# Two attention-and-MLP layers on one core: opening loads reordered, q/k drains shared between two engines, and rules in the instruction scheduler meant to keep ScalarE fed

## The chip, the cores and the metric

The kernel runs on one core of a Trainium2 chip. The metric is the device time of one execution in microseconds (us). A median is taken over the executions of one kernel; "span" is the length of the one execution that was profiled, some 2 us shorter than its time. Engine names: PE is TensorE (matmuls), ACT is ScalarE, DVE is VectorE, POOL is GpSimd, SP is the engine that issues most DMA transfers.

## The reference, cut to what matters

A sequence of 2048 tokens of width 576 passes two layers. Each is sliding-window attention (32 heads of 18, window 256), then an MLP of 4608 hidden units with tanh-gelu, both behind a layer norm and with a residual.

```python
def _A_ref(x, wqkv, wo):                        # attention
    H = 32; Dh = D // H; W = 256
    q, k, v = ...                               # x @ wqkv, split into heads
    scores = jnp.einsum("bhqd,bhkd->bhqk", q, k) * (Dh ** -0.5)
    scores = jnp.where(mask, scores, -1e9)      # causal, at most 256 back
    o = jnp.einsum("bhqk,bhkd->bhqd", _softmax(scores), v)
    return o.reshape(B, S, D) @ wo
def _B_ref(x, w1, b1, w2, b2):                  # MLP
    h = _gelu(x @ w1 + b1)
    return h @ w2 + b2
for _ in range(2):                              # two layers, same weights
    x = x + _A_ref(_layernorm(x), ...)
    x = x + _B_ref(_layernorm(x), ...)
```

## The kernel before

The work is cut into eight chunks of 512 tokens, four per layer. A chunk passes these stages: projections to q, k and v (120 matmuls), eight head groups of scores, exp, mask and weighted sum, the output projection (40 matmuls), a first MLP half and a second MLP half. I call the hidden half of a chunk a gelu block: there are 16 of them, two per chunk, and their order is fixed. Stages of different chunks overlap: while ACT works on one chunk's exps, PE multiplies for another.

The program does not write instructions directly. It adds tasks with an engine, a cost in us, a priority, and what they read and write. A greedy scheduler then places them by a model of time and thereby fixes each engine's instruction order. The kernel hands each engine its instructions in that order, so what waits in a list holds up what stands behind it (the profile after shows DVE standing 3.54 us in this way).

```python
while len(order) < n:                           # Plan.schedule, cut
    best = None
    for e in ENGS:
        for t in released[e]:
            st = max(free[e], t.ready)
            if t.alloc:                         # banks of PSUM it needs
                got, when = place(t)
                ...
                st = max(st, when)
            key = (round(st, 3), t.prio, t.idx) # earliest start first, then priority
            if best is None or key < best[0]:
                best = (key, t, st, got)
    _, t, st, got = best
    if t.eng == "pe" and st < self.warm_until and st - free["pe"] > 0.4:
        self.keep_warm(free["pe"], st, bank_free, extra)   # dummy matmuls into the gap
    ...
```

Scores and exps of one unit (a head group has three units after the first chunk). The scores of four heads fill two pairs of PSUM banks, of which three are open to them; each pair is emptied by one exp on ACT:

```python
add("pe", fn, reads=rd, writes=bs, cost=0.06 + ncol * 0.00053, ..., alloc=bs, fifo="pa", after=[...])
for h2 in range(2):
    add("act", lambda e, h2=h2: e.activation(pT[...], two(bs[h2])[:, :, lo:hi], ACT.Exp, scale=SCALE), ..., fifo="act", prio=prio)
...                                             # masks on POOL, then the weighted sum on PE
```

The opening, for chunk 0. A q or k tile is drained from PSUM in two halves by DVE and then turned by a DMA transpose; the scores wait for those transposes. The value weights, the second chunk's input and the two MLP biases are loaded while this goes on. The 18 KB bias b1 is read element by element into a column layout:

```python
w_load(0); w_load(1)                            # q and k weights; v follows below
for i in range(n0):
    ln_rstd([i], False, -20)
    ln_norm_T(i, i, xnTa, "xa", -6, x_in, [f"xin{i}"], pe=True)
dma("pool", b2bc[:, :], ..., reads=["xa3"], writes=["b2"], ...)
def load_b1(e):
    src = bass.AP(tensor=B_b1.tensor, offset=B_b1.offset, ap=[[1, P], [P, NF], [1, 1]])
    ... e.dma_start(b1col[:, :], src)
add("pool", load_b1, reads=["xa3"], writes=["b1"], dma="b", ...)
w_load(2, ["xa0"])                              # value weights
xin_load(4, 4, ["xa0"], -6)                     # input of the second chunk
for i in range(n0):
    qkv(0, i, -5)
xin_load(8, 4, ["k3"], -4)                      # input of the third chunk

# in qkv: drains of a q or k tile
for o in range(2):
    add("dve", ... e.tensor_copy(qv[:, o * 16:(o + 1) * 16, 0:DH], bank(b)...), reads=[bs[o]], writes=[f"qn{sl}h{o}"], cost=0.42, prio=prio)
add("sp", ... e.dma_start_transpose(dst, qn[:, sl, :]), reads=[f"qn{sl}h0", f"qn{sl}h1"], ...)
```

The softmax here doesn't subtract the row's maximum and nothing guards it: scores larger than these inputs give would overflow.

## Time and profile before

| | before |
|---|---|
| time at the time of the prediction | 958.56 us, median of 3 |
| span of the profiled run | 953.9 us |
| PE busy | 914.3 us |
| ACT busy, 25.8 us (first exp) to 110.3 us (first gelu block) | 58.1 of 84.5 us |
| dummy matmuls | 71 |

First the page's table of busy time (us, share of the span, instructions), its PE part:

```profile
PE 914.3 (96%) x9403; PEld 564.0 (59%) x9403; DVE 313.7 (33%) x804; ACT 590.7 (62%) x709; POOL 369.1 (39%) x507
```

PE is the limit of the kernel as a whole. The Trainium skill, "Trainium Kernel Development and Optimization", section Performance Expectations, calls matmul busy time a bad metric for the distance to the limit, because matmuls are pipelined.

Next the waits of ACT, from the first exp to the first gelu block. The columns are who waited, for whom, us in total, times, and the longest:

```profile
ACT pT L655 <- PE ps L646: 38.6, 27, 12.2
```

12.2 of these 38.6 us lie before the first exp; the other 26.4 are the idle time between exps, always for scores. Then, in the timeline of PE just before the first gelu block (start, us, engine, line, what), the dummies of line 490:

```profile
105.62 1.01 PE L490 MATMUL ps<-warm 128*128 128x256 bf16 x4
...
107.56 1.16 PE L490 MATMUL ps<-warm 128*128 128x256 bf16 x7
108.65 0.40 PE L646 MATMUL ps<-x_res,kT 32*128 32x256 bf16 x8
...
110.27 0.61 PE L771 MATMUL ps<-xnTm,w_sb 64*128 64x512 bf16 x4
```

All projections that could be done were done (400, of which 40 are output projections), so PE waited for exps and ran dummies. They did not hold the full clock: it was 0.69 in 105 to 110 us. The late start of the exps stands in the first exp, in the first score matmul's wait, and in the DMA queues from 8 to 26 us (packets, MB, share of 16 engines; below, issues with KB and median us to landing):

```profile
25.79 1.51 ACT L655 ACTIVATE pT<-ps 128x768 bf16<-128x768 f32 x2 [12.24 <-PE ps L646]
```

```profile
25.40 0.34 PE L646 MATMUL ps<-qT,kT 32*128 32x384 bf16 x4 [2.78 <-DMA qT<-qn]
```

```profile
q0 software_dynamic: 4768, 0.31, 79.8%
...
qT<-qn SPq DMA_TRANSPOSE x4, 5.5
...
b1col<-in_B_b_dram POOLq DMA_DIRECT2D x1, 18.0 KB, 10.3
```

The packets of 0.31 MB of biases, 4768 of them, are under way for 80% of the DMA engines' time in this stretch. Shares of different queues overlap: the hardware queue has 77.1% in the same stretch. Last, the granted PE clock in two stretches of the opening. The columns are stretch, length, then busy us and instructions of PE, PEld, DVE, ACT and POOL, then the clock (0.91 and 0.83), DMA share and GB/s:

```profile
20.00:40.00 20.00, 14.27 (x164) 9.09 (x162) 12.50 (x36) 10.16 (x14) 8.20 (x12) 0.91 1.55 138
40.00:60.00 20.00, 17.77 (x239) 11.17 (x236) 9.63 (x23) 13.74 (x19) 13.69 (x21) 0.83 0.92 191
```

### The profile page before, as it was taken

To read this page: it belongs to the slowest core of one execution; us is meant where nothing else is said; L and a number is where in the kernel's file an instruction comes from. 1 tells how busy PE (TensorE), PEld (TensorE's weight loads), DVE (VectorE), ACT (ScalarE), POOL (GpSimd) and SP (SyncE) were. 2 spreads that over 40 slices of the span, in tenths; PEclk is the share of its full clock that TensorE was granted. 3 is DMA by queue.
4 is the path that set the end of the run, shared out by engine and by line. 5 is a ranking of instruction groups with operands and counts; after the bars stand their busy time and mean duration, and the time that the engine had idled before them with its cause. 6 is when DMAs were issued, how large, how long until landed. Compare 5 with 4: busy or idle time off the path is not lost. (4 is left out here: it accounts for less than half of the span.)

```text
span 953.9 us, 22759 instructions
## 1 busy us (share of the span) xinstructions
PE 914.3 (96%) x9403; PEld 564.0 (59%) x9403; DVE 313.7 (33%) x804; ACT 590.7 (62%) x709; POOL 369.1 (39%) x507
## 2 busy tenths in 40 slices
PE   8799899999999999999999999999999999999998
PEld 6466455564664746655575656747466464656556
DVE  7556301461153412723145221442215220241001
ACT  1676768476836778376744877557784677752541
POOL 4555636164531636225331544315443163620100
PEclk9799999999999999999999999999999999999999
DMA  9898456954098340984259351983519816174540
GB/s 198 145 217 143 96 171 179 200 129 123 27 201 201 93 126 14 219 177 138 75 119 201 90 168 46 176 175 89 182 26 189 193 47 191 36 202 131 161 137 26
DMA packets 240663, 130.10 MB, mean 136 GB/s; under 512 B 158768, under 2 KB 238384, under 8 KB 240560
## 3 DMA queue, kind: packets, MB, share of 16 engines
q1 hardware_dynamic: 231248, 120.96, 54.3%
q0 software_dynamic: 6880, 5.03, 3.5%
q10 hardware_dynamic: 2432, 2.65, 0.9%
q8 instruction: 75, 1.23, 0.5%
q14 instruction: 28, 0.23, 0.1%
HBM read 91.87 MB, written 2.36 MB: 99 GB/s over the span
## 5 line engine op out<-in xcount | busy, mean ns | idle before, releaser
L655 ACT ACTIVATE pT<-ps 128x1024 bf16<-128x1024 f32 (+2 forms) x384 | 347.8, 971 | 118.1 <-PE ps L646 116.9
L676 POOL TENSOR_SCALAR_AFFINE_SELECT pT<-pT 128x512 bf16<-128x512 bf16 (+1 forms) x368 | 278.7, 781 | 278.4 <-ACT pT L655 262.4
L786 ACT ACTIVATE hT<-ps,b1col 128x512 bf16<-128x512 f32 x288 | 197.9, 687 | 215.8 <-PE ps L783 215.1
L811 PE MATMUL ps<-w_sb,hT 128*128 128x288 bf16 x2304 | 314.3, 286 | 4.3 <-DVE x_res L727 2.7
L783 PE MATMUL ps<-xnTm,w_sb 128*128 128x512 bf16 x1152 | 267.3, 381 | 0.0
L811 PEld LDWEIGHTS ps<-w_sb,hT 128*128 128x128 bf16 x2304 | 210.9, 97 | 79.5 <-issue 19.2
L783 PEld LDWEIGHTS ps<-xnTm,w_sb 128*128 128x128 bf16 x1152 | 105.9, 98 | 141.1 <-issue 28.7
L727 DVE TENSOR_TENSOR x_res<-ps,x_res 128x288 f32<-128x288 f32 x160 | 70.6, 449 | 349.3 <-PE ps L811 328.9
L580 PE MATMUL ps<-wqkv,xnTa 128*128 128x288 bf16 x960 | 135.0, 290 | 4.7 <-DVE qn L610 2.0
L580 PEld LDWEIGHTS ps<-wqkv,xnTa 128*128 128x128 bf16 x960 | 88.8, 99 | 37.5 <-DVE qn L610 5.4
L693 PEld LDWEIGHTS ps<-vA,pT 128*128 128x128 bf16 x2880 | 95.0, 96 | 26.2 <-issue 9.4
L693 PE MATMUL ps<-vA,pT 128*128 128x20 bf16 x2880 | 100.0, 172 | 4.3 <-POOL pT L676 2.7
L793 POOL TENSOR_TENSOR x_res<-x_res,b2bc 128x576 f32<-128x576 f32 x32 | 44.9, 1402 | 93.7 <-ACT hT L786 93.7
L646 PE MATMUL ps<-qT,kT 32*128 32x384 bf16 (+2 forms) x1216 | 64.6, 278 | 8.5 <-ACT pT L655 4.8
L610 DVE CAST qn<-ps 128x288 bf16<-128x288 f32 x128 | 58.1, 455 | 39.0 <-PE ps L580 37.9
L512 POOL TENSOR_SCALAR vtmp<-mv_all 128x1 f32<-128x1 f32 (+1 forms) x43 | 8.3, 192 | 142.7 <-DVE mv_all L503 142.2
L580 PE MATMUL ps<-wo_sb,attT 128*128 128x288 bf16 x320 | 42.7, 286 | 7.8 <-DMA attT<-attq 6.5
L501 DVE BATCH_NORM_STATS2 st_all<-x_res 128x6 f32<-128x288 f32 x104 | 44.8, 447 | 13.8 <-DMA x_res<-in_A_x_dram 12.7
L771 PE MATMUL ps<-xnTm,w_sb 64*128 64x512 bf16 x288 | 45.0, 381 | 2.3 <-ACT pT L655 2.2
L730 DVE TENSOR_TENSOR xn<-ps,x_res 128x288 bf16<-128x288 f32 x32 | 14.6, 458 | 97.4 <-PE ps L811 97.4
L646 PEld LDWEIGHTS ps<-qT,kT 32*128 32x128 bf16 x1216 | 19.6, 92 | 39.6 <-issue 23.2
L524 DVE TENSOR_SCALAR xn<-x_res,mv_all,rstd 128x576 bf16<-128x576 f32 x52 | 31.6, 610 | 34.0 <-DMA xnTm<-xn 23.0
(38 smaller groups left out, 278.2 us busy)
## 6 DMA issues: line engine op xcount, KB each, us to landing
w_sb<-in_B_w_dram SPq DMA_DIRECT2D x144, 288.0 KB, 4.9
w_sb<-in_B_w_dram SPq DMA_DIRECT2D x72, 512.0 KB, 4.2
w_sb<-in_B_w_dram SPq DMA_DIRECT2D x144, 32.0 KB, 3.7
x_res<-in_A_x_dram POOLq DMA_DIRECT2D x4, 1152.0 KB, 7.9
out_dram<-xn SPq DMA_DIRECT2D x16, 144.0 KB, 1.8
wqkv<-in_A_wqkv_dram ACTq DMA_DIRECT2D x3, 576.0 KB, 5.3
hT<-in_A_x_dram SPq DMA_DIRECT2D x2, 576.0 KB, 4.0
wo_sb<-in_A_wo_dram ACTq DMA_DIRECT2D x1, 576.0 KB, 4.4
```

Of the source, the lines that this page charges most:

```text
L580: ins = e.matmul(bank(bs[o])[:, 0:HB], lhs(c), rhs(c, o * HB), start=(c == 0), stop=(c == KD - 1))
L610: add("dve", lambda e, o=o, b=bs[o], qv=qv: e.tensor_copy(qv[:, o * 16:(o + 1) * 16, 0:DH], bank(b)[:, 0:HB].rearrange("p (h d) -> p h d", ...
L646: ins = e.matmul(two(bs[j // 2])[:, j % 2, col:col + nq * 128], k_of(T0 + so)[0][32 * j:32 * j + 32, g, :], qs[32 * j:32 * j + 32, g, qo * ...
L655: add("act", lambda e, h2=h2: e.activation(pT[:, sl, 2 * h2:2 * h2 + 2, lo:hi], two(bs[h2])[:, :, lo:hi], ACT.Exp, scale=SCALE), reads=[bs ...
L676: add("pool", lambda e, ap=ap, pat=pat, sgn=sgn, kind=kind: e.affine_select(ap, ap, pattern=pat, compare_op=(ALU.is_ge if kind == "d" else ...
L693: ins = e.matmul(bank(B_O)[:, o:o + VW], pT[:, sl, j, col + qi * 128:col + (qi + 1) * 128], vA[:, (T0 + so) % VS, 4 * g + j, :], start=(fi ...
L727: add("dve", lambda e: e.tensor_tensor(x_res[:, t, sl], bank(b)[:, 0:HB], x_res[:, t, sl], ALU.add), reads=[b], writes=[f"x{t}h{hh}"], cos ...
L771: ins = e.matmul(bank(bk)[:, 0:n], w1_sb[64 * b:64 * b + 64, sl, col:col + 128], xnTm[64 * b:64 * b + 64, k % 2, 4, 0:n], start=True, stop ...
L783: ins = e.matmul(bank(bk)[:, 0:n], w1_sb[:, sl, col:col + 128], xnTm[:, k % 2, c, 0:n], start=False, stop=(c == 3))
L786: add("act", lambda e, ff=ff, fl=fl, bk=bk: e.activation(hT[:, fl, 0:n], bank(bk)[:, 0:n], ACT.Gelu_apprx_tanh, bias=b1col[:, ff:ff + 1]), ...
L793: add("pool", lambda e, t=t: e.tensor_tensor(x_res[:, t, :], x_res[:, t, :], b2bc[:, :], ALU.add), reads=["b2", f"h{fs[0]}"], writes=X(t), ...
L811: ins = e.matmul(bank(b)[:, 0:HB], hT[:, fl, i * 128:(i + 1) * 128], w2_sb[:, fl, hh * HB:(hh + 1) * HB], start=(fl == 0), stop=(fl == NFH ...
```

## The change

Intent: let the exps start earlier and keep ACT supplied with scores in the first 75 us of the plan, so that the first gelu block need not wait for them. Parts, which I call the moves and the rules:

- Moves: value weights are loaded at once; both biases wait for the last k transpose (`k3`); the second chunk's input waits for `xa3` instead of `xa0`; every second half-drain of q and k in chunk 0 goes to ACT. The planned landing time of chunk 0's transposes rises from 2.5 to 4.5 us, one large memset is held back, and the copies of the opening's PE transposes leave the fixed order of ACT's tasks (not in the cut below).
- Rules: before placing a PE task that is not a score, the scheduler asks whether it would make the next score late enough to let ACT run dry (`starves`), and then takes another candidate. A gelu block may go first if it can start within 0.3 us (`hold`). A score unit is planned 0.08 us dearer. The value projections of the second chunk get a later priority.

```diff
+        def starves(t, st, got):
+            if fed == len(feed) or feed[fed].npred:
+                return False
+            f = feed[fed]
+            where, when = place(f)
+            ...
+            at = max(free["pe"], f.ready, when)
+            end = st + t.cost
+            late = end if at < end else at
+            if ...:                              # t takes a bank that f wants
+                late = max(late, end + 0.65)
+            return late > at and late + f.cost + f.lat > max(free["act"], st) + backlog
...
+            if t.eng == "pe" and t.fifo is None and st < self.feed_until and starves(t, st, got):
+                for c in sorted(cands, key=lambda c: c[0]):
+                    if c[1].fifo is not None or not starves(*c[1:]):
+                        _, t, st, got = c
+                        break
+            if t.eng == "pe" and t.fifo is None:
+                for c in cands:
+                    if c[1].hold and c[2] <= st + self.hold:
+                        _, t, st, got = c
...
+FEED_UNTIL = 75.0
+HOLD = 0.3
...
+    w_load(2)
...
-            prio = prio0 if k else QK0.get((w, i), -0.55 + 0.01 * i)
+            prio = prio0 + (0.8 if k == 1 and w == "v" else 0.0) if k else QK0.get((w, i), -0.55 + 0.01 * i)
...
+                    if k == 0 and o == 1:
+                        add("act", lambda e, b=bs[o], dst=dst: e.copy(dst, bank(b)[:, 0:HB]...), ..., cost=0.45, lat=0.2, prio=prio)
+                    else:
+                        add("dve", ...)
...
-        add("pe", fn, ..., cost=0.06 + ncol * 0.00053, ...)      # scores
+        add("pe", fn, ..., cost=0.14 + ncol * 0.00053, ...)
...
-            add("pe", rest, ..., cost=mm_cost(n) * (n4 // 2) + 0.21, prio=prio, ...)
+            add("pe", rest, ..., cost=mm_cost(n) * (n4 // 2) + 0.21, hold=True, prio=prio, ...)
...
-    dma("pool", b2bc[:, :], ..., reads=["xa3"], ...)             # and load_b1 likewise
-    w_load(2, ["xa0"])
-    xin_load(4, 4, ["xa0"], -6)
+    xin_load(4, 4, ["xa3"], -6)
     for i in range(n0):
         qkv(0, i, -5)
+    dma("pool", b2bc[:, :], ..., reads=["k3"], ...)              # and load_b1 likewise
```

Since the scheduler is greedy, each of these edits shifts the instruction order far beyond its own place. Before the first gelu block the new order has 365 projection matmuls in place of 400.

More of the change, by code (lines that the diff above doesn't have):

```diff
@@ L159 @@
     __slots__ = ("idx", "eng", "fn", "reads", "writes", "cost", "lat", "prio", "dma", "ring", "handles", "alloc", "move",
-                 "npred", "succ", "ready", "end", "plain")
+                 "npred", "succ", "ready", "end", "plain", "fifo", "hold", "stage")
     def __init__(self, **kw):
@@ L196, in __init__, with add @@
         self.warm_until = 0.0
+        self.feed_until = 0.0
+        self.hold = 0.0
+        self.stage = ""
+        self.nudge = {}
         self.fifo_last = {}
-    def add(self, eng, fn, reads=(), writes=(), dma=None, ring=4, cost=0.1, lat=0.1, prio=0.0, alloc=(), fifo=None, plain=False, after=(), move=0.0):
+    def add(self, eng, fn, reads=(), writes=(), dma=None, ring=4, cost=0.1, lat=0.1, prio=0.0, alloc=(), fifo=None, plain=False, after=(), move=0.0, hold=False):
+        prio += self.nudge.get(self.stage, 0.0)
         t = Task(idx=len(self.tasks), eng=eng, fn=fn, reads=tuple(reads), writes=tuple(writes), cost=cost, lat=lat, prio=prio,
                  dma=dma, ring=ring, alloc=tuple(alloc), handles=tuple({r for r in tuple(reads) + tuple(writes) if isinstance(r, Bank)}),
-                 plain=plain, move=move)
+                 plain=plain, move=move, fifo=fifo, hold=hold, stage=self.stage)
         pred = set()
@@ L244, in keep_warm @@
         t = Task(idx=-1, eng="pe", fn=lambda e: self.warm_fn(e, h.no, n), reads=("warm",), writes=(h,), cost=n * 0.115, lat=0.1, prio=0.0,
-                 dma=None, ring=4, alloc=(), handles=(), plain=False, move=0.0)
+                 dma=None, ring=4, alloc=(), handles=(), plain=False, move=0.0, fifo=None, hold=False, stage="")
         extra.append((a, t))
@@ L275, in place @@
             return got, when
+        feed = [t for t in self.tasks if t.fifo == "pa"]
+        fed = 0
+        backlog = 0.0
+        def starves(t, st, got):
[3 more added lines that the diff above has]
+            where, when = place(f)
+            if where is None:
+                return False
+            at = max(free["pe"], f.ready, when)
+            end = st + t.cost
+            late = end if at < end else at
+            if t.alloc and set(got) & {b for w, h in zip(where, f.alloc) for b in ((w, w + 1) if h.pair else (w,))}:
+                late = max(late, end + 0.65)
+            return late > at and late + f.cost + f.lat > max(free["act"], st) + backlog
         order = []
@@ L282, in schedule @@
             best = None
+            cands = []
             for e in ENGS:
@@ L292, in schedule @@
                     key = (round(st, 3), t.prio, t.idx)
+                    if e == "pe" and st < self.feed_until or t.hold:
+                        cands.append((key, t, st, got))
                     if best is None or key < best[0]:
@@ L305, in schedule @@
             free[t.eng] = st + t.cost
+            if t.fifo == "pa":
+                fed += 1
+                backlog += sum(x.cost for x, data in t.succ if data and x.eng == "act")
+            elif t.fifo == "act" and t.handles:
+                backlog -= t.cost
             if t.dma is not None:
@@ L477, in build_kernel @@
     add("pool", lambda e: e.memset(xn[:, :, D:KD * 128], 0.0), writes=[f"xn{i}" for i in range(NXN)], cost=0.4, prio=-10)
-    add("pool", lambda e: e.memset(vA[:, :, :, DH:VW], 1.0), writes=[f"v{s}h{h}" for s in range(VS) for h in range(2)], cost=1.6, prio=-8)
     for i in range(NQN):
@@ L494, in build_kernel @@
     PL.warm_until = WARM_UNTIL
+    PL.feed_until = FEED_UNTIL
+    PL.hold = HOLD
     def ln_stats(t, prio, src=None, srcres=None):
@@ L542, in ln_norm_T @@
             add("act", lambda e: e.copy(dst[:, :, i * 128:(i + 1) * 128], bank(b).bitcast(BF16)[:, 0:KD * 128].rearrange("p (c q) -> p c q", c=KD)),
-                reads=[b], writes=[f"{dname}{i}"], cost=0.75, lat=0.2, prio=prio, fifo="act")
+                reads=[b], writes=[f"{dname}{i}"], cost=0.75, lat=0.2, prio=prio)
             return
@@ L609, in qkv @@
                 for o in range(2):
-                    add("dve", lambda e, o=o, b=bs[o], qv=qv: e.tensor_copy(qv[:, o * 16:(o + 1) * 16, 0:DH],
-                                                                          bank(b)[:, 0:HB].rearrange("p (h d) -> p h d", d=DH)),
-                        reads=[bs[o]], writes=[f"qn{sl}h{o}"], cost=0.42, prio=prio)
+                    dst = qv[:, o * 16:(o + 1) * 16, 0:DH]
+                    if k == 0 and o == 1:
+                        add("act", lambda e, b=bs[o], dst=dst: e.copy(dst, bank(b)[:, 0:HB].rearrange("p (h d) -> p h d", d=DH)),
+                            reads=[bs[o]], writes=[f"qn{sl}h{o}"], cost=0.45, lat=0.2, prio=prio)
+                    else:
+                        add("dve", lambda e, b=bs[o], dst=dst: e.tensor_copy(dst, bank(b)[:, 0:HB].rearrange("p (h d) -> p h d", d=DH)),
+                            reads=[bs[o]], writes=[f"qn{sl}h{o}"], cost=0.42, prio=prio)
                 if w == "q":
@@ L618, in qkv @@
                 add("sp", lambda e, dst=dst, sl=sl: e.dma_start_transpose(dst, qn[:, sl, :]),
-                    reads=[f"qn{sl}h0", f"qn{sl}h1"], writes=[dn], dma="t", ring=8, cost=1.3, lat=2.5, move=0.6, prio=prio)
+                    reads=[f"qn{sl}h0", f"qn{sl}h1"], writes=[dn], dma="t", ring=8, cost=1.3, lat=2.5 if k else 4.5, move=0.6, prio=prio)
     def units_of(k):
@@ L650, in scores @@
         ncol = sum(p[2] for p in parts) * 128
-        add("pe", fn, reads=rd, writes=bs, cost=0.06 + ncol * 0.00053, prio=prio, lat=0.15, alloc=bs, fifo="pa", after=[f"p{sl}h{h}" for h in range(2)] + [f"p{sl}m{m}" for m in range(3)])
+        add("pe", fn, reads=rd, writes=bs, cost=0.14 + ncol * 0.00053, prio=prio, lat=0.15, alloc=bs, fifo="pa", after=[f"p{sl}h{h}" for h in range(2)] + [f"p{sl}m{m}" for m in range(3)])
         lo = min(p[3] for p in parts)
@@ L773, in rest @@
                 return ins
-            add("pe", rest, reads=rd, writes=bks, cost=mm_cost(n) * (n4 // 2) + 0.21, prio=prio, alloc=bks, fifo="pa",
+            add("pe", rest, reads=rd, writes=bks, cost=mm_cost(n) * (n4 // 2) + 0.21, hold=True, prio=prio, alloc=bks, fifo="pa",
                 after=[f"h{ff - hf * NFH}" for ff in fs])
@@ L843, in build_kernel @@
         ln_norm_T(i, i, xnTa, "xa", -6, x_in, [f"xin{i}"], pe=True)
-    dma("pool", b2bc[:, :], bass.AP(tensor=B_b2.tensor, offset=B_b2.offset, ap=[[0, P], [1, D]]), reads=["xa3"], writes=["b2"], cls="b", ring=2,
+    add("pool", lambda e: e.memset(vA[:, :, :, DH:VW], 1.0), writes=[f"v{s}h{h}" for s in range(VS) for h in range(2)], cost=0.7, reads=["rstd3"], prio=-5)
+    xin_load(4, 4, ["xa3"], -6)
+    for i in range(n0):
+        qkv(0, i, -5)
+    dma("pool", b2bc[:, :], bass.AP(tensor=B_b2.tensor, offset=B_b2.offset, ap=[[0, P], [1, D]]), reads=["k3"], writes=["b2"], cls="b", ring=2,
         cost=1.0, prio=-1)
@@ L850, in load_b1 @@
             return e.dma_start(b1col[:, :], src)
-    add("pool", load_b1, reads=["xa3"], writes=["b1"], dma="b", ring=2, cost=2.0, lat=10.0, prio=-1)
-    w_load(2, ["xa0"])
-    xin_load(4, 4, ["xa0"], -6)
-    for i in range(n0):
-        qkv(0, i, -5)
+    add("pool", load_b1, reads=["k3"], writes=["b1"], dma="b", ring=2, cost=2.0, lat=10.0, prio=-1)
     xin_load(8, 4, ["k3"], -4)
@@ L883, in build_kernel @@
             if 1 < k < NK - 1:
+                PL.stage = f"ln{k + 1}"
                 ln1(k + 1, b + 1)
+            PL.stage = f"ea{k}"
             E(k, range(0, CUT.get(k, 4)), b - 0.5)
+            PL.stage = f"ld{k}"
             if k == 0:
@@ L891, in build_kernel @@
         if k >= 2:
+            PL.stage = f"mb{k - 2}"
             mm2(k - 2, 1, b)
@@ L894, in build_kernel @@
         if k >= 1:
+            PL.stage = f"ga{k - 1}"
             G_part(k - 1, 0, b + 1)
@@ L898, in build_kernel @@
         if not last:
+            PL.stage = f"eb{k}"
             E(k, range(CUT.get(k, 4), 8), b + 1.5)
+            PL.stage = f"le{k}"
             if k == 0:
@@ L908, in build_kernel @@
         if k >= 1:
+            PL.stage = f"ma{k - 1}"
             mm2(k - 1, 0, b + 2)
@@ L913, in build_kernel @@
                 for i in range(CH[k + 1][2]):
+                    PL.stage = f"q{k + 1}.{i}"
                     qkv(k + 1, i, b + 2.2 + 0.2 * i)
             if k == 0:
+                PL.stage = f"ln2"
                 ln1_in(2, 1)
+            PL.stage = f"t{k}"
             tail(k, b + 1.9)
@@ L920, in build_kernel @@
         if k >= 1:
+            PL.stage = f"gb{k - 1}"
             G_part(k - 1, 1, b + 3)
+    PL.stage = f"mb{NK - 1}"
     mm2(NK - 1, 1, b + 4)
```

## The prediction

> **What bounds it now.** By the busy table TensorE (PE) works 914.3 of 953.9 us; from 140 us on the stretches show it at 94 to 99%. Only the opening is loose. From 0 to 140 us PE is idle 16 us and spends 12.3 us on dummy warm-up matmuls (line table), 7 us of them before the first input landed. ScalarE (ACT) decides this stretch: from 25.8 us (first exp) to 110.3 us (first gelu-stage matmul) it is busy 58.1 of 84.5 us, and its waits there are all on score matmuls. The exps of one head group cost 4.5 us (timeline). Because they started late and were fed unevenly, PE ran out of other work at 100 to 110 us: waits on exp, plus 17 dummies. A second exp-bound gap sits at 154 to 160 us.
>
> **Why late.** The first score matmul (25.4 us) waited 2.8 us for a transpose of q. In 8 to 26 us the DMA table gives the software queue (the two bias loads) 80% of the DMA engines' time for 0.31 MB; the 18 KB bias took 10.3 us, and a q transpose 5.5 us to land where 3.0 is the least. The Trainium skill, "DMA: Bandwidth & Descriptors", arbitration, says each DMA engine takes turns between queues packet by packet; the trace agrees: tiny packets ahead of transposes. VectorE alone drained the 16 q/k banks at 0.46 us each, until 21.3 us.
>
> **What changes.** No real matmul goes away; dummies 71 to 70. (1) Value weights (648 KB) move into the opening burst: q/k weights may land up to 1 us later. (2) Bias loads wait for the last k transpose, so q/k transposes should land in 3 to 4 us. They then meet the second chunk's input transposes: 1 to 2 us lost. (3) Eight drains of about 0.45 us (estimated from exps: 0.6 us for 512 columns, 0.81 for 768) go to idle ACT; VectorE finishes 3 us sooner. PE still has 95 projection matmuls before the first scores: these start at 22.5 to 24 us. (4) The instruction order now puts scores first, with one or two projection tiles between: before the first gelu-stage matmul stand 365 projection matmuls instead of 400 (4.3 us deferred).
>
> **Sum.** Exps until the first gelu stage need 59 us. At 90% feeding (between 30.7 and 47.9 us the old kernel reached 88%) they end near 90 us instead of 110. The 20 us minus 4.3 is 15.5 us. The deferred work fills later gaps (154 to 160 us, the attention transposes' wait near 178 us): 2 to 3 us more. Minus 1 for contention. After 200 us PE is full; reordering there, and the rule that lets a gelu block go first, I take as plus or minus 4 us.
>
> Predicted 942 us, eight times in ten within 932 to 953. Faster by over 2% (below 939.4): 0.35; within 2%: 0.62; slower: 0.03.
>
> **What would show it.** First exp at 22.5 to 24 us; ACT idle from there to the first gelu-stage matmul 5 to 9 us instead of 26; that matmul at 88 to 93 us; no dummies at 100 to 110; PE busy total 900 to 913 us; after 200 us the same pace.
>
> **What would make it wrong.** A late first projection because three weight loads share the queues; biases delaying the second chunk's transposes so that PE, in order, stands and ACT starves; the masks on GpSimd (about 3.7 us per group, estimated from 0.5 us per block) becoming the limit; a drain that keeps PSUM banks; more cold-clock time (granted 0.83 at 40 to 60 us); later stages losing what the opening wins, or gaining beyond it.

## More of the kernel before

The chain of waits shows what the matmuls need when they follow each other without pause (start, us, what; the number after x counts matmuls):

```profile
768.56 0.39 PE ps L693 x16
768.95 0.33 PE ps L646 x8
...
860.33 17.64 PE ps L811 x144
877.97 0.54 PE ps L771 x4
878.50 3.56 PE ps L783 x16
```

That is 0.0244 us for a weighted-sum matmul, 0.041 for a score (a mean over units that differ in columns), 0.1225 for one with 288 columns (projections, output projections, second MLP matrix), 0.135 and 0.2225 for the two kinds of the first MLP matrix. With 0.072 for each of the 20 transposes on PE (ten took 0.72 us), and times the counts of the program, this makes 863.7 us of matmul work, an estimate, and the same before and after the change, for no real matmul is added or removed. I call the difference between a moment and the work done until then the loss. The kernel loses about 90 us in all, far more than the 40 us in which the table has PE idle. This measure, which I formed only after the prediction, tells where a gain arises even when the order of work changes.

## The result, and the profile after

| | before | after |
|---|---|---|
| time, median of 6 | 957.16 us (953.32 to 961.03) | 944.33 us (943.53 to 946.01) |
| ratio after/before | | 0.987 (95% interval 0.9841 to 0.9899) |
| span profiled | 953.9 us | 942.4 us |
| first exp | 25.79 us | 22.39 us |
| first gelu block | 110.27 us | 102.71 us |
| ACT idle between the two | 26.4 us | 22.3 us |

A ratio is worked out from the fast runs of both kernels in the same rounds, so it is not quite the ratio of the medians that stand beside it. The change is a gain of 1.3%, clear of noise, and below 2%.

The table of busy time, and the waits of ACT from 22 us to the first gelu block (2.0 of the 23.9 us lie before the first exp):

```profile
PE 906.8 (96%) x9353; PEld 563.4 (60%) x9402; DVE 312.2 (33%) x796; ACT 592.3 (63%) x717; POOL 369.5 (39%) x507
```

```profile
ACT pT L704 <- PE ps L695: 23.9, 18, 3.4
```

```profile
102.71 0.61 PE L820 MATMUL ps<-xnTm,w_sb 64*128 64x512 bf16 x4
```

The last line is the first gelu block, from PE's timeline. Some records are missing from this trace: of the 1152 matmuls of one kind (L832) it has 1103, so PE's busy time is somewhat short. Run 6, which has the same order and all records, shows 911.9 us.

DMA, again from 8 to 26 us: the software queue with the biases is gone from this stretch, and a q transpose lands in 3.8 us.

```profile
qT<-qn SPq DMA_TRANSPOSE x4, 3.8
kT<-qn SPq DMA_TRANSPOSE x4, 3.3
```

The timeline of ACT shows where it is now fed. From 63.8 to 81.0 us it works almost without a gap. Then the rule ends, and gaps come back:

```profile
22.39 1.51 ACT L704 ACTIVATE pT<-ps 128x768 bf16<-128x768 f32 x2 [2.02 <-PE ps L695]
...
63.76 4.39 ACT L704 ACTIVATE pT<-ps 128x1024 bf16<-128x1024 f32 x6 [0.30 <-PE ps L695]
68.45 12.54 ACT L704 ACTIVATE pT<-ps 128x1024 bf16<-128x1024 f32 x14 [0.31 <-PE ps L695]
82.34 1.94 ACT L704 ACTIVATE pT<-ps 128x1024 bf16<-128x1024 f32 x2 [1.35 <-PE ps L695]
87.71 1.94 ACT L704 ACTIVATE pT<-ps 128x1024 bf16<-128x1024 f32 x2 [3.43 <-PE ps L695]
```

The longest waits of PE up to 140 us, and what PE and DVE did at the one of 2.8 us:

```profile
PE ps L625 <- DVE qn L660: 4.5, 8, 1.4
PE ps L695 <- ACT pT L704: 2.8, 5, 1.2
PE ps L742 <- DVE mv_all L548: 2.8, 1, 2.8
```

```profile
34.77 1.18 DVE L546 BATCH_NORM_STATS2 st_all<-hT 128x6 f32<-128x288 bf16 x3 [3.54 <-DMA hT<-in_A_x_dram]
```

```profile
36.99 0.47 PE L742 MATMUL ps<-vA,pT 128*128 128x20 bf16 x12 [2.79 <-DVE mv_all L548]
...
39.61 1.36 PE L625 MATMUL ps<-wqkv,xnTa 128*128 128x288 bf16 x5
```

DVE stood before the statistics of the third chunk's input, which had not landed; the division of a head group stood behind them in DVE's list, and PE's next weighted sum needed that division. After the pause five projection matmuls take 1.36 us; as many take 0.79 us elsewhere. The Trainium skill, "TensorE: Matmul & The Clock Gate", Part 1, says that PE's clock falls to half after an idle window and comes back after a busy one; the trace agrees with the half rate: the granted clock is 0.50 from about 36 us on, still within the pause, and is back at 1.00 by 50 us. The pause was shorter than the page has it; the last section comes back to this. The two stretches, to be held against those of before (clock 0.90 and 0.76 now):

```profile
20.00:40.00 20.00, 14.50 (x184) 9.06 (x182) 13.10 (x41) 11.31 (x16) 11.76 (x16) 0.90 1.44 149
40.00:60.00 20.00, 17.15 (x219) 10.27 (x216) 10.09 (x22) 13.89 (x20) 13.74 (x20) 0.76 1.01 195
```

Where did the gain arise? The times of the landmarks are read from PE's timeline, the work done by then is the estimate described above, and the loss is the difference:

| landmark | before: time, work, loss | after: time, work, loss | loss saved so far |
|---|---|---|---|
| first score matmul | 25.4, 13.1, 12.3 | 22.0, 13.1, 8.9 | 3.4 |
| first gelu block | 110.3, 70.6, 39.7 | 102.7, 66.3, 36.4 | 3.3 |
| third gelu block | 220.7, 170.4, 50.3 | 208.3, 166.1, 42.2 | 8.1 |
| seventh gelu block | 443.0, 381.2, 61.7 | 434.2, 381.2, 52.9 | 8.8 |
| end | 953.9, 863.7, 90.2 | 942.4, 863.7, 78.7 | 11.5 |

Between the first score and the first gelu block, where for the most part the rule is on, PE loses as much as before (27.4 and 27.5 us). The gain lies ahead of it (3.4 us), behind it up to the third gelu block (4.8 us), and a rest after (3.4 us). In the middle stretch the gaps that the prediction had named have shrunk: PE's waits for exps fall from 2.8 to 1.7 us, its wait of 1.6 us for the attention transposes is gone, and the mean granted clock rises from 0.98 to 1.00.

### The profile page after: what moved, and what is told of

It is laid out like the page before. It is cut to its first block, busy times and chain, and to the rows that moved or that the text cites. A ratio compares the mean times of both kernels' runs of the same rounds, so it can differ in the third digit from the quotient of the medians.

```text
span 942.4 us, 22728 instructions
## 1 busy us (share of the span) xinstructions
PE 906.8 (96%) x9353; PEld 563.4 (60%) x9402; DVE 312.2 (33%) x796; ACT 592.3 (63%) x717; POOL 369.5 (39%) x507
## 5 line engine op out<-in xcount | busy, mean ns | idle before, releaser
L832 PE MATMUL ps<-xnTm,w_sb 128*128 128x512 bf16 x1103 | 259.5, 379 | 3.4 <-issue 1.1
L860 PEld LDWEIGHTS ps<-w_sb,hT 128*128 128x128 bf16 x2304 | 211.4, 97 | 75.0 <-issue 16.6
L832 PEld LDWEIGHTS ps<-xnTm,w_sb 128*128 128x128 bf16 x1152 | 107.1, 98 | 132.1 <-issue 20.1
L742 PEld LDWEIGHTS ps<-vA,pT 128*128 128x128 bf16 x2880 | 92.9, 96 | 33.2 <-issue 14.6
L660 DVE CAST qn<-ps 128x288 bf16<-128x288 f32 x120 | 54.2, 455 | 47.7 <-PE ps L625 47.4
L695 PEld LDWEIGHTS ps<-qT,kT 32*128 32x128 bf16 x1216 | 19.5, 92 | 36.1 <-issue 17.9
```

The source lines that it names most:

```text
L660: add("dve", lambda e, b=bs[o], dst=dst: e.tensor_copy(dst, bank(b)[:, 0:HB].rearrange("p (h d) -> p h d", d=DH)), reads=[bs[o]], writes=[ ...
L695: ins = e.matmul(two(bs[j // 2])[:, j % 2, col:col + nq * 128], k_of(T0 + so)[0][32 * j:32 * j + 32, g, :], qs[32 * j:32 * j + 32, g, qo * ...
L742: ins = e.matmul(bank(B_O)[:, o:o + VW], pT[:, sl, j, col + qi * 128:col + (qi + 1) * 128], vA[:, (T0 + so) % VS, 4 * g + j, :], start=(fi ...
L832: ins = e.matmul(bank(bk)[:, 0:n], w1_sb[:, sl, col:col + 128], xnTm[:, k % 2, c, 0:n], start=False, stop=(c == 3))
L860: ins = e.matmul(bank(b)[:, 0:HB], hT[:, fl, i * 128:(i + 1) * 128], w2_sb[:, fl, hh * HB:(hh + 1) * HB], start=(fl == 0), stop=(fl == NFH ...
```

## The experiments

Theory P, from the prediction: feeding ACT is the gain; the exps end earlier, so the gelu block comes earlier. Theory Q, from the table above: the exps only start earlier, the rule gains nothing on the way, and later gains come from hold or from chance. Further theories came up on the way. Each run had 5 rounds except where noted. Loss values are from the profiled run of each kernel, in the order first, third, seventh gelu block and end. Nine of the kernels traced here, the changed one among them, have the same matmul order up to the first score and reach it between 21.8 and 23.4 us (the slow execution of run 1 aside), so I take a loss difference below 2 us to mean nothing.

### 1. The feeding rule off

```diff
-FEED_UNTIL = 75.0
+FEED_UNTIL = 0.0
```

> The changed kernel with the feeding rule switched off (its time limit set to 0), everything else kept. Theory 1 (the prediction's main term: the rule feeds ScalarE and is worth most of the gain): ScalarE's idle time between the first exp and the first gelu-stage matmul grows from 21 us to 26 us or more, that matmul comes at 107 us or later instead of 102.7, and the time is 949 us or more. Theory 2 (the opening gained only because the first scores came 3.4 us earlier; between first score and first gelu-stage matmul both kernels lose 27 us beyond their real matmul work): the first exp stays at 22.4 us, and the time stays within 943 to 946 us.

Measured: 950.26 us median of 6; ratio 0.9923 (0.9901 to 0.9945). One execution, the profiled one, took 1464.69 us at a granted clock of 0.556; it is left out of the ratio.

> The same kernel as the run without the feeding rule, for a profile in the fast state (the first fell in a state with granted clock 0.556). Theory 1 (the rule feeds ScalarE): first exp at 22 to 24 us as with the rule, but first gelu-stage matmul at 107 to 110 us instead of 102.7, and ScalarE idle 26 us or more between the two. Theory 2 (the 6 us come from elsewhere): that matmul at 102 to 105 us and the loss after 170 us.

Measured: 948.62 us in one run (its granted clock, 0.995, is like that of the fast ones). First exp at 23.83 us; ACT idle 26.2 us from there to the first gelu block; that block at 107.8 us, with dummies before it again:

```profile
104.49 1.16 PE L533 MATMUL ps<-warm 128*128 128x256 bf16 x9
105.90 0.40 PE L695 MATMUL ps<-x_res,kT 32*128 32x256 bf16 x8 [0.25 <-ACT pT L704]
...
107.82 0.61 PE L820 MATMUL ps<-xnTm,w_sb 64*128 64x512 bf16 x4 [0.18 <-ACT pT L704]
```

Losses: 37.3, 48.7, 58.7, 83.2 against 36.4, 42.2, 52.9, 78.7 with the rule. So the order that the rule makes is worth about 6 us of 944, and theory Q's second half falls. But it doesn't pay where it acts: at the first gelu block the two stand within 0.9 us of loss. It pays between the first and the third block (11.4 us lost without, 5.8 with). Without the rule all 400 projections are done by the first gelu block; with it 35 are left over and stand in the list where PE would wait later.

### 2. The hold rule off

```diff
-            add("pe", rest, ..., + 0.21, hold=True, prio=prio, ...)
+            add("pe", rest, ..., + 0.21, prio=prio, ...)
```

> The changed kernel without the rule that lets a gelu block go first (hold), feeding rule kept. Of the 11.5 us gained 5.8 are there by 170 us and 5.7 come later, where only hold, the new cost of a score block and the shifted order act. Theory 1 (hold makes the late gain): 948 to 951 us, and equal up to 100 us. Theory 2 (the late gain comes from the deferred projections that fill gaps, or is luck of the order): 943 to 946 us.

Measured: 943.46 us median of 5; ratio 0.9848 (0.9824 to 0.9871). That is no slower than the full change, 0.987 (0.9841 to 0.9899); the intervals overlap, so it can't be called faster either. Losses 36.0, 41.4, 54.0, 79.7. Hold is not needed for the gain.

### 3. All rules undone, the moves kept

```diff
-FEED_UNTIL = 75.0
+FEED_UNTIL = 0.0
...                          # hold=True, the 0.14 and the 0.8 also undone
```

> The changed kernel with all its scheduler changes undone (no feeding rule, no hold, old cost of a score block, old priority of the second chunk's value projections); kept are the loads moved and the eight drains on ScalarE. Theory 1 (the scheduler rules carry the gain): 953 us or more, though the first exp still comes at 22.4 us. Theory 2 (the moved loads and drains carry the opening's gain of 3.4 to 5.8 us): 950 to 954 us if late gains need the rules, 944 to 947 us if the moved loads and drains are the whole cause.

Measured: 955.77 us median of 6 (950.92 to 962.75, a wide spread); ratio 0.9992 (0.9957 to 1.0027). The first exp came at 23.30 us, 2.5 us earlier than in the kernel before, and nothing was gained: the first gelu block stands at 111.1 us. These landmarks are from the profiled run, which was the slowest of the six, so I read no losses from it.

### 4. The rules alone, the moves undone

```diff
-    w_load(2)
+    w_load(2, ["xa0"])      # at its old place, and xin_load(4, 4, ["xa0"], -6)
...
-reads=["k3"]                # both biases
+reads=["xa3"]
...
-                    if k == 0 and o == 1:
+                    if False:
```

The planned landing time and the fixed order of ACT's copies are set back too; the held-back memset stays, as it does in run 3.

> The kernel before with only the scheduler's changes (feeding rule, hold, score cost 0.14, value projections of the second chunk later); value weights, bias loads, second input load and drains as before. The run with the moved loads and drains alone came out at 955.8 us, no gain over before, and the one without the feeding rule at 950.3. Theory 1 (the rules carry the whole gain): 943 to 946 us, with the first exp still at about 25.5 us. Theory 2 (the rules only pay when the first scores also come early; the two parts need each other): 948 to 954 us.

Measured: 953.11 us median of 6 (947.66 to 957.24); ratio 0.9945 (0.9915 to 0.9975). Losses 43.6, 51.2, 61.5, 87.9. Its first score waited still longer than in the kernel before:

```profile
27.73 0.51 PE L694 MATMUL ps<-qT,kT 32*128 32x384 bf16 x4 [7.57 <-DMA qT<-qn]
```

With runs 3 and 4 the four corners are there: neither 1, moves alone 0.9992, rules alone 0.9945, both 0.987. The product of the single ratios would be 0.9937. Both together are below even the lower end of the interval of the rules alone (0.9899 at most against 0.9915 at least). So the two together give more than the product of their parts, as theory 2 of this run had it. The margin is thin: the gap of 0.0067 to the product stands against an uncertainty of about 0.0054 (an estimate: the half widths of the three intervals, added in squares). And the rules alone do gain 0.55%.

### 5. The old cost of a score unit

```diff
-cost=0.14 + ncol * 0.00053
+cost=0.06 + ncol * 0.00053
```

> The changed kernel with the scheduler's old cost of a score block (0.06 us instead of 0.14 plus the columns), feeding rule and all else kept. Without the feeding rule the time was 950.3 us, without any scheduler change 955.8 us; the hold rule was worth nothing (943.5 without it), so the new cost or the later value projections should hold the other 5 us. Theory 1 (the cost does it, by a truer plan of ScalarE's feeding): 947 to 950 us. Theory 2 (it is the value projections, or chance of the order): 943 to 946 us.

Measured: 946.73 us median of 6; ratio 0.9878 (0.9855 to 0.9902), not to be told from the full change. The cost is not needed. What makes up the 5 us between runs 1 and 3 (hold, cost and later value projections together, with the rule off) I did not separate.

### 6. The bias load without its packets, after the change

The 4608 single elements become 128 runs of 72 bytes. The bias is then permuted, so the result is wrong. All engines keep their instruction order, so this run is free of the scheduler's chance.

```diff
-        src = bass.AP(tensor=B_b1.tensor, offset=B_b1.offset, ap=[[1, P], [P, NF], [1, 1]])
+        src = bass.AP(tensor=B_b1.tensor, offset=B_b1.offset, ap=[[NF, P], [1, NF]])
```

> The changed kernel, instruction order the same on all engines; only the 18 KB bias is read in 128 runs of 72 bytes instead of 4608 single elements, which permutes the bias: the result is wrong on purpose. Theory 1 (the held-back bias load now jams the DMA queues from 27 to 41 us, so the input of the third chunk lands late, VectorE stands before it for 3.5 us, and TensorE and ScalarE with it): the bias lands in under 5 us instead of 13.6, the 2.8 us wait of TensorE near 34 us is gone, the first gelu-stage matmul comes 3 to 4 us earlier, time 940 to 942 us. Theory 2 (TensorE's own work sets the pace there): within 1 us of the changed kernel.

Measured: 944.42 us median of 6; ratio 0.9866 (0.9842 to 0.989). The bias landed in 4.7 us instead of 13.6. Yet DVE stood as long before the third chunk's input, which landed 7.3 us after its issue (6.8 before the edit), and PE as long behind DVE:

```profile
36.62 1.18 DVE L546 BATCH_NORM_STATS2 st_all<-hT 128x6 f32<-128x288 bf16 x3 [3.95 <-DMA hT<-in_A_x_dram]
```

```profile
38.85 0.45 PE L742 MATMUL ps<-vA,pT 128*128 128x20 bf16 x12 [3.19 <-DVE mv_all L548]
```

So my suspicion that the 18 KB bias jams the queue and makes this pause is refuted. What delays that input is not found; the other bias (288 KB) and the transposes of the second chunk's input were under way beside it and stayed as they were.

### 7. The third chunk's input later

```diff
-    xin_load(8, 4, ["k3"], -4)
+    xin_load(8, 4, ["aq0"], -4)
```

> The changed kernel with the input load of the third chunk held until the first head group's output is done, instead of the last k transpose. In the changed kernel VectorE, which runs in order, stood 3.5 us before this load with the division of a head group queued behind it; TensorE then stood 2.8 us near 34 us, and its granted clock fell to 0.76 in 40 to 60 us. Making the 18 KB bias land early (4.7 us instead of 13.6) changed nothing of that. Theory 1 (VectorE's place in the queue is the cause, and the cold clock follows from it): the wait is gone, the clock in 40 to 60 us is above 0.9, and the time is 938 to 941 us. Theory 2 (something else, ScalarE or the order of TensorE, then takes over the wait): 943 to 946 us.

Measured: 950.31 us median of 6; ratio 0.9917 (0.9887 to 0.9947), slower than the full change. The wait for the statistics is gone from PE's list, and others stand in its place (PE's waits up to 110 us):

```profile
PE ps L625 <- DVE qn L660: 3.8, 5, 2.1
PE ps L742 <- DVE attq L757: 1.9, 1, 1.9
PE ps L742 <- POOL pT L725: 1.7, 2, 1.5
```

The clock in 40 to 60 us was 0.83, not above 0.9. The loss at the first gelu block was 38.4 us against 36.4, and the new order put all 400 projections ahead of that block again. The run is not a clean test of the pause, because the scheduler answered the edit with another order; but theory 1 as I wrote it fell. The run is a warning, too: it has all the moves and rules, and one dependency on an input load cost 6 us, as much as the rule is worth. So a draw of the greedy order can be of that size. Runs 2 and 5, two more orders with both parts, came within 3 us of the full change, which speaks for the rule; but how far the time scatters over orders was not measured, and chance of the order stays a rival.

### 8. The leftover projections without the rule

Could one get the gain of run 1 by holding back projections by hand? The feeding rule is off; the projections of the third chunk's last tile wait for the second chunk's last head group.

```diff
-                         [f"w{w}A", f"w{w}B", f"w{w}C", f"xa{i}"], ...
+                         [f"w{w}A", f"w{w}B", f"w{w}C", f"xa{i}"] + (["aq7"] if k == 2 and i >= 3 else []), ...
```

> The changed kernel without the feeding rule, but with the projections of the third chunk's last tile (30 matmuls) held by a dependency until the second chunk's attention is done, so that 370 instead of 400 projection matmuls stand before the first gelu-stage matmul, as with the rule (365). In the traces the rule's gain shows as 4.3 us of projections moved behind that matmul, where they fill gaps of TensorE. Theory A (where the projections stand is the whole of it; the rule is only a way to put them there): 943 to 946 us. Theory B (ScalarE must be ahead as well, or TensorE only idles before the first gelu stage instead of after it: exps end at 107 us as before): 948 to 951 us, as without the rule, with the first gelu-stage matmul still at 105 to 108 us and more dummy matmuls before it.

Measured: 950.58 us median of 6; ratio 0.9929 (0.9907 to 0.9951), the same as without the rule (0.9923). 370 projections stand before the first gelu block, and it comes at 106.3 us; 47 dummies run between 22 and 110 us instead of 40 in run 1 and 27 in the full change. Losses 39.4, 49.0, 59.9, 84.9: with the projections moved, PE loses 39.4 us up to the gelu block (37.3 in run 1) and 9.6 from there to the third block (11.4 there, 5.8 in the full change). So it is not the place of the projections that counts by itself. That ACT has to be ahead as well, so that PE may leave them, is the likely reading; no run shows it alone.

### 9. The feeding rule for longer

```diff
-FEED_UNTIL = 75.0
+FEED_UNTIL = 110.0
```

> The changed kernel with the feeding rule's time limit at 110 us of the plan instead of 75; 320 projection matmuls (instead of 365) stand before the first gelu-stage matmul. In the changed kernel ScalarE is fed without a gap from 63 to 81 us and then waits 8 us in gaps up to 101 us, after the rule has ended. Theory 1 (the rule works as long as it is on): ScalarE's idle time between first exp and first gelu-stage matmul falls from 21 us to 15 us or less, that matmul comes at 96 to 98 us, and with gaps left to fill after it the time is 939 to 942 us. Theory 2 (the gaps behind are full already: between 103 and 208 us the changed kernel loses only 5.5 us beyond its matmul work): that matmul comes earlier but the time is 943 to 946 us.

Measured: 954.95 us median of 6; ratio 0.9976 (0.9951 to 1.0001). The first gelu block came at 101.1 us with 320 projections done, and ACT's idle time up to it was 19.5 us. But the loss there was 39.9 us, more than the 36.4 of the full change: 1.6 us were saved and 5.2 us of work put off. Then the debt came due. After the second chunk's exps PE works off 75 projection matmuls in one stretch from 152.5 us, and in ACT's timeline the gelus wait 11 us (in the full change the first of them follows the table load at once, at 154.64 us):

```profile
150.41 1.28 ACT L876 ACT_TABLE_LOAD   x1
162.74 0.69 ACT L835 ACTIVATE hT<-ps,b1col 128x512 bf16<-128x512 f32 x1 [11.05 <-PE ps L832]
```

Losses at the third block, seventh block and end: 49.9, 63.3, 87.5. Both theories of this run fell: more feeding brings the gelu block 1.6 us forward and has lost 8.8 us more than the full change by the end.

### 10. The bias load without its packets, before the change

The edit of run 6 in the kernel before, instruction order unchanged.

> The kernel before, instruction order the same on all engines; only the 18 KB bias is read in 128 runs of 72 bytes instead of 4608 single elements (result wrong on purpose). Theory 1 (the bias's packets held up the transposes of q in 14 to 26 us): the last-needed q transpose lands 2 to 3 us earlier, the first exp comes at 23 to 24 us instead of 25.8, time 954 to 955 us. Theory 2 (the transposes are slow by themselves, or by the value weights and the second input load): first exp at 25 to 26 us, time within 1.5 us of the kernel before.

Measured: 955.42 us median of 6; ratio 0.998 (0.9953 to 1.0007). The first exp came 3.0 us earlier, and the median q transpose landed in 4.4 us instead of 5.5:

```profile
22.80 1.51 ACT L655 ACTIVATE pT<-ps 128x768 bf16<-128x768 f32 x2 [9.45 <-PE ps L646]
```

So the bias's packets did hold up the transposes, as predicted (the same edit in run 11 brings the first exp 2.3 us forward), and as the Trainium skill ("DMA: Bandwidth & Descriptors", section Queues, rings and completion order) lets one expect of queues that take turns by packet. But the next wait took most of it back (PE's second group of scores waited 2.6 us for a k transpose), and the first gelu block gained 0.8 us.

### 11. The same edit with the rules alone

> The kernel with the scheduler's rules alone (953.1 us, first score waiting 7.6 us for a transpose of q, the 18 KB bias landing in 13.9 us), instruction order the same on all engines; only the bias is read in 128 runs of 72 bytes instead of 4608 single elements (result wrong on purpose). In the kernel before the same edit brought the first exp from 25.8 to 22.8 us and the time by only 0.2 per cent. Theory 1 (with the rules on, an early start of the exps is worth its full length; the bias's packets are the part of the moved loads that counts): first exp at 22.5 to 24 us, time 944 to 948 us. Theory 2 (the early start is absorbed as in the kernel before; the other moves, drains on ScalarE and early value weights, are needed): first exp early too, but time 950 to 953 us.

Measured: 950.8 us median of 6; ratio 0.994 (0.9916 to 0.9964), no different from the rules alone (0.9945). The first exp came at 26.0 instead of 28.3 us; the first score still waited 5.4 us for a q transpose. The condition that both theories named, an exp at 22.5 to 24 us, was not met. So it stays open which of the moves (bias, value weights, second input, drains) brings the rest. They were not undone one by one in the full change.

No version clearly beats the change. The one without hold (943.46 us) ties with it.

## Why the prediction was right, point by point

The time: 942 us predicted, 944.33 measured, inside 932 to 953 and in the class given the greatest chance (within 2%). The gain was 12.8 us (medians) where 16.6 had been predicted from a kernel before at 958.56. The mechanism was right in outline: the loss sat in the opening and was ACT waiting for scores, early transposes and scores first both mattered, and work left over filled later gaps. The sizes of the terms were not.

- **First exp at 22.5 to 24 us.** 22.39 us, 0.1 us below the range. The cause given, bias packets in front of q transposes, is shown for the kernel before by run 10, where it alone brings 3.0 us; what the other moves add was not separated (run 11). Alone it is worth next to nothing in the end (runs 3 and 10).
- **"At 90% feeding they end near 90 us."** This is the step that failed. ACT was fed 58.0 of 80.3 us, 72%, against 69% before; idle 22.3 us where 5 to 9 were predicted. The first gelu block came at 102.7 us, not 88 to 93. I had taken the best stretch of the old kernel as the mark for a whole of 65 us, and had not asked whether PE could deliver. In the traces PE loses 27 us between first score and first gelu block with and without the change: pauses, half clock (0.76 in 40 to 60 us), and 27 dummies after 22 us. When run 9 fed ACT longer, PE only fell behind.
- **"15.5 us" up to the first gelu block.** The block came 7.6 us earlier with 4.3 us of work left over, which makes 3.3 us.
- **"2 to 3 us more" from later gaps.** 4.8 us by the third gelu block. They are the gaps that the prediction named. Run 1 ties this to the feeding rule and run 8 shows that moving the projections alone doesn't bring it.
- **"Plus or minus 4" after 200 us.** 3.4 us gained between the third gelu block and the end. Within what I allowed; not explained. The rules reorder everything there, and I found no single part of the change that owns it (hold doesn't, run 2).
- **No dummies at 100 to 110 us; PE busy 900 to 913 us.** Right: the last dummy starts at 74.2 us, and PE is busy 906.8 us (911.9 in run 6, which has all records).
- **Named risks.** A pause of PE with its cold clock did occur, by the third chunk's input and DVE's order. The bias was not its cause (run 6). The masks on POOL did not become the limit: PE's waits up to 140 us have 0.2 us for them.

So the sum came out near by luck: one term was far too large (15.5 for 3.3) and two were too small (2 to 3 for 4.8, 0 for 3.4). Runs 3 and 4 show what the prediction didn't see: moves and rules are not two terms of a sum. The early start alone pays nothing that is clear of noise (0.9992), the rules alone less than half of the gain (0.9945). That this is the work of feeding, and not in part of the luck of one greedy order, is argued and not shown (run 7).

## What to carry to other kernels

When two engines feed each other, an earlier start on one can be lost again at the next wait, as in runs 3 and 10; test such parts in the four corners (neither, each, both) before crediting either. Measure a stage by time minus work done, not by busy share or by the time of one landmark, since a scheduler can pull a landmark forward by leaving work behind. And do not set the pace of an engine from its best stretch: ask what its supplier loses on the same stretch.

## What the Trainium skill lacked or had wrong

- "TensorE: Matmul & The Clock Gate", Part 1, puts the fall to half rate at an idle window of about 3.4 us or more. Here the granted clock fell to 0.50 within an idle stretch of 2.79 us, less than 2 us after the last matmul had ended (34.2 and about 36 us), and five projection matmuls took 1.36 us instead of 0.79 near 39.6 us. In the kernel before they take 1.38 us at 41.1 and 44.4 us, with no single PE pause over 1.13 us between 30 and 41 us. Thin activity was enough there. The same Part tells of short idles between groups of matmuls that make the clock swing, but not how thin the activity must be.
- "DMA: Bandwidth & Descriptors", section DMA Transpose (X-bar), gives constraints and alternatives, and the page elsewhere a bandwidth, but no time from issue to landing. Here a transpose of q or k took 3.0 us at best; those of q in the opening took 3.8 in the median with the biases held back, 5.5 beside the bias load in the kernel before, and 7.0 in the kernel with the rules alone.
- The same page's arbitration by packet fits what 4608 element-sized pieces did to transposes in one place (3.0 us earlier exp without them, run 10). It doesn't tell when such a load is harmless, as it was in run 6, where the neighbouring 576 KB load took 6.8 us with the pieces and 7.3 without.
- No page has the state in which one execution of run 1 took 1464.69 us at a granted clock of 0.556 on a single core, while five others took 949 to 952 us. In its trace the clock stays at 0.55 to 0.56 from 20 us to the end.
